# A spectral layer followed by an MLP on one core: prologue and first stages in another order, with products of zeros on TensorE

## The chip, the cores and the metric

The kernel runs on one core of a Trainium2 chip. The metric is the device time of one launch in microseconds (us), the median of several runs. TensorE (PE) multiplies matrices, VectorE (DVE), ScalarE (ACT) and GpSimd (POOL) work on elements, and SyncE (SP) issues transfers; each engine has an instruction queue of its own, in order, and waits for others by semaphores.

## The reference

Eight sequences of 3008 tokens with 256 features go through a linear layer in the frequency domain and then through an MLP. All results are float32; the weights of the MLP come as float64.

```python
X = np.fft.rfft(x, axis=1)
Xr, Xi = (X.real.astype(np.float32), X.imag.astype(np.float32))
Yr = Xr @ w_r - Xi @ w_i + b_r
Yi = Xr @ w_i + Xi @ w_r + b_i
lam = 0.01
Yr = np.sign(Yr) * np.maximum(np.abs(Yr) - lam, 0.0)
Yi = np.sign(Yi) * np.maximum(np.abs(Yi) - lam, 0.0)
Y = Yr.astype(np.float64) + 1j * Yi.astype(np.float64)
y = np.fft.irfft(Y, n=x.shape[1], axis=1)
...
h = x @ w_in
g = np.maximum(0.01 * h, h)
return (g @ w_out).astype(np.float32)
```

In the MLP x is y as 24064 tokens; w_in is 256 x 2048 and w_out 2048 x 256.

## The kernel before

**The transforms.** A transform of 3008 = 47 x 64 points is two stages of products with constant matrices. `fwd(b)` is stage A of batch b: it loads x in seven blocks ("chunks"; the tile is xin), adds and subtracts its two halves (`fold`, tile xs; DVE for batch 0, POOL later), multiplies by fa, copies the result to SBUF and stores it to DRAM as u_dram. `mid(b)` is the middle part: for 12 pairs of frequencies it loads u, does stage B (product with fb, L335), the linear layer (`proj`: three products with w_r, w_i - w_r and -(w_r + w_i), called wr, wd, wn), the threshold (tiles t and c), a copy with signs (zf), and the first stage of the inverse with gb (`stage_g`, here called the turn), and stores v_dram. `inverse` loads vin, multiplies by ga (L472), and gives y as chunks of 512 tokens (yc).

**The MLP ("MoE" in the names).** There are 47 chunks of tokens with 8 steps q each. It multiplies by a scheme of seven products in place of eight; `forms(ci)` makes its operands yh and yl out of yc (tile yt holds differences), as a rounded part and the rest. `moe_a` and `moe_b` multiply with w_in (`block`, L84: hi*hi, hi*lo, lo*hi), put the seven products together (p, u, gf) and apply the slope, and `moe_o` (L568) multiplies gh and gl with w_out two steps later. From batch 2 on the transforms are done with such split operands too: `split` in `fwd` makes xz, and `split_consts` splits wr, wd, wn, gb and fa into hi and lo (L104, L105). Batches 0 and 1 do stage A in plain float32, and batch 0 also the middle part.

**The weights.** w_in is loaded raw (win_raw) in four quarters (`load_win`) and turned to float32 by `convert_win`, 13 instructions on DVE for each; w_out is done in eight pieces by `load_wout`.

**The order.** Ahead of the MoE, `fwd(0)` runs, then `mid(0)` with the conversions of w_in laid between its steps, then `fwd(1)`, then the inverse and `forms` of chunk 0. The rest runs inside the MoE: a `Stream` is a generator with a total of columns, and `to(frac)` takes it on as far as the position in the MoE asks. The MoE is cut into stretches, numbered cur = 0 to 6, one for each middle part that remains; a stretch holds the streams in turn. Before, stretch cur has `fwd(cur + 2)` and then `mid(cur + 1)`, so that u of a batch is stored one stretch before it is read. `load(j)` at the start of `mid` fetches the first two u pairs.

**What sets an engine's order.** The program is written in one order for all engines, and a scheduler of the framework puts each engine's instructions in a row by its own simulated time; `tc.issue_after(ins)` adds an edge to that. Tiles of one tag share buffers; psh, psf and pso are the PSUM banks.

Of the kernel before, what the change touches and what calls it, by code (L numbers as in the profile page):

```python
# [8 lines left out]
F32 = mybir.dt.float32  # L9
# [9 lines left out]
N1, N2, NK1 = 47, 64, 24  # L19
# [11 lines left out]
def spectral_mlp_kernel(  # L31
# [171 lines left out]
    reads, written, turned, turning, thresholded = [], [], [], [], []  # L203
    NX = -(-NS // 2)
    XT = [("gf", 2)] + [("gl", 2)] * 2 + [("gh", 2)] * 2 + [("yc", 2)] * 2
    XT1 = [("yc", 2)] * 2 + [("gf", 2), ("gh", 2), ("yl", 2), ("yh", 2), ("gh", 2)]

    def fwd(b):
# [3 lines left out]
        x_t, s_t = {}, {}  # L212

        def load(c):
            cols = slice(2 * c * D, min(2 * c + 2, NS) * D)
            n = cols.stop - cols.start
            if b < NPRE:
                tag, bufs = (XT, XT1)[b][c]
                x2 = sb.tile([PA, 2, 2 * D], F32, name="xin", tag=tag, bufs=bufs)
                x_t[c] = [x2[:, h, :n] for h in range(2)]  # L220
            else:
                x_t[c] = [
                    sb.tile([PA, 2 * D], F32, name=f"xin{h}", tag="uv"[h], bufs=3 - h)[:, :n] for h in range(2)
                ]
            for h, t in enumerate(x_t[c]):
                if b == 0:
                    (act if h else sync).dma_start(t, x[b, h, :, cols])
                else:
                    with tc.issue_after(reads[-1].ins):
                        sync.dma_start(t, x[b, h, :, cols])  # L230
# [19 lines left out]
        def stage_a(c, h):  # L250
            t = x_t[c][h]
            n = t.shape[1]
            pa = (bank("psf", 2) if b else bank("psh", 4))[:PA, :n]
            products(pa, [(consts[f"fa{h}"] if b else consts[f"fa{h}32"], s_t[c][h])])
            t = x_t[c][1 - h]
            cp = act.copy(t, pa)
            if b == 0:
                turned[:] = [cp]
            st = (act if b else sync).dma_start(uv[h, :, 2 * c * D:2 * c * D + n], t)
            if b == 0:  # L260
                written.append(st)
# [22 lines left out]
        ahead = 2 if b >= NPRE else NX  # L284
        for c in range(ahead):
            load(c)
# [17 lines left out]
    def mid(b):  # L304
# [111 lines left out]
        yield 0  # L416
# [71 lines left out]
    def forms(ci):  # L488
# [7 lines left out]
        def split(k, w):  # L496
            act.copy(yh[:, k], w)  # L497
            return dve.tensor_sub(yl[:, k], w, yh[:, k].bitcast(F32))  # L498
# [12 lines left out]
        if ci == 0:  # L511
            made[:] = [last]
# [126 lines left out]

    fa32 = sb.tile([PA, 3, PA], F32, name="fa32", tag="xi", bufs=1)  # L640
# [7 lines left out]
    load_win(0, (sync, act))  # L648
    load_plain("fb", fb, [P, NK1 + 1, N2])
    load_weights()  # L650
# [6 lines left out]
    sync.dma_start(consts["gb32"][0], gb)  # L657
# [6 lines left out]
    load_win(1, (sync, sync), written[7])  # L664
# [4 lines left out]
    act.copy(bz[:1], brow[:1])  # L669
    act.copy(bz[32:33], brow[32:33])  # L670
    dve.tensor_sub(bz[32:33], brow[32:33], bz[32:33].bitcast(F32))
    act.mul(fa32[:, 2], fa32[:, 1], -1.0)
    convert_win(0)
    m0 = Stream(mid(0), MID)
    m0.to(0.001)
    for c in range(2, 4):
        load_win(c, (sync, sync), reads[3])
# [6 lines left out]
    with tc.issue_after(turned[0].ins):  # L684
        convert_win(1)
    wout = load_wout()
    for i in range(1, 17):
        m0.to(i / 16)
        if i in (3, 8):
            convert_win(2 + i // 8)  # L690
# [4 lines left out]
    m0.finish()  # L695
    fp.to(0.69)
# [5 lines left out]
    with tc.issue_after(thresholded[-1].ins):  # L702
        split_consts()
# [3 lines left out]
    next(wout)  # L707


    mids = [Stream(mid(b), MID) for b in range(1, NB)]  # L710
    cur, streams = -1, ()
    for i, pos in enumerate(moe()):
# [3 lines left out]
        if i in (2, 4):  # L716
            with tc.issue_after(made[0].ins):
                next(fp.gen)
        while cur + 1 < NB - 1 and pos >= (read[cur + 1] if cur >= 0 else 0):
# [3 lines left out]
            streams = ([Stream(fwd(cur + NPRE), FWD)] if cur + NPRE < NB else []) + [mids[cur]]  # L723
# [111 lines left out]
```

## Time and profile before

| | before |
| --- | --- |
| median of 3 runs | 2609.61 us (2607.25 to 2610.03) |
| profiled execution | 2609.83 us |
| its span, first to last instruction | 2608.0 us |
| PE busy | 2543.3 us (98%) |
| DVE busy | 1884.8 us (72%) |
| ACT busy | 1654.5 us (63%) |
| mean granted clock of TensorE | 0.991 |

The span is what the trace covers; 1.8 us of the execution lie outside it. PE idles for 64.7 us in all. The granted clock is a share of the full 2.4 GHz, so that 0.5 is the lower of the two levels. A window of the trace gives, for a stretch of time, how long each engine was busy and how many instructions it had.

### The profile page before, as it was taken

How to read it: one execution, taken by the hardware profiler on the slowest of the kernel's cores; microseconds unless marked ns; L12 is line 12 of the kernel's file. 1: busy time of each engine (PE TensorE's matmuls, PEld its weight loads, DVE VectorE, ACT ScalarE, POOL GpSimd, SP SyncE). 2: the span in 40 equal slices, each digit the busy share in tenths (PEclk: the TensorE clock that was granted, in tenths of full speed). 3: DMA queues.
4: the chain of work that ended last, by engine and by line, in shares of the span. 5: the costliest groups of instructions: out<-in, count | busy, mean ns of one | idle time of the engine just before them, and what ended most of it. 6: DMA issues, size and time to landing. Idle time of an engine off the chain costs nothing.

```text
span 2608.0 us, 42647 instructions
## 1 busy us (share of the span) xinstructions
PE 2543.3 (98%) x16300; PEld 2283.9 (88%) x16300; DVE 1884.8 (72%) x3403; ACT 1654.5 (63%) x3174; POOL 248.2 (10%) x180
## 2 busy tenths in 40 slices
PE   5899999999999999999999999999999999999999
PEld 3678887999989999899999999999999999989998
DVE  6697667777787777777777777777777767667665
ACT  4665665676656666567665766666666666655554
POOL 0002102100120001200021000211000000000000
PEclk8999999999999999999999999999999999999999
DMA  8634113211142112312123111231111111100000
GB/s 248 172 99 116 53 42 92 84 52 47 32 120 61 48 37 56 101 53 59 33 74 94 52 45 41 74 94 52 45 41 53 41 41 44 42 18 32 9 17 17
DMA packets 119914, 165.14 MB, mean 63 GB/s; under 512 B 13602, under 2 KB 69918, under 8 KB 119710
## 3 DMA queue, kind: packets, MB, share of 16 engines
q1 hardware_dynamic: 79120, 115.55, 14.5%
q10 hardware_dynamic: 40589, 46.87, 7.1%
q8 instruction: 128, 2.10, 0.3%
q14 instruction: 77, 0.62, 0.1%
HBM read 86.60 MB, written 75.76 MB: 62 GB/s over the span
## 4 chain that ended last, share of the span: by engine, by line
PE 90%; DVE 3%; ACT 3%; DMA 1%; issue 1%; ACTq 0%; SPq 0%; DVEq 0%
PE pso L568 38%; PE psh L84 34%; PE psf L78 11%; PE psf L472 3%; PE psf L335 3%; DVE gl L555 1%; ACT zf L392 0%; ACT gh L553 0%; ACT gf L551 0%; DMA u_dram<-xin 0%; DVE yl L498 0%; ACT zf L388 0%; DMA raw<-w_out_dram 0%; DVE gf L549 0%; ACTq L412 0%
## 5 line engine op out<-in xcount | busy, mean ns | idle before, releaser
L84 PE MATMUL psh<-yh,win_hi 128*128 128x256 f32 x2632 | 738.4, 285 | 8.1 <-ACT yh L497 4.1
L84 PE MATMUL psh<-yl,win_hi 128*128 128x256 f32 x2632 | 735.1, 281 | 0.0
L84 PE MATMUL psh<-yh,win_lo 128*128 128x256 f32 x2632 | 727.2, 280 | 0.0
L555 DVE TENSOR_TENSOR gl<-gf,gh 128x1024 fp32r<-128x1024 f32 x376 | 475.9, 1266 | 197.5 <-ACT gh L553 195.9
L568 PE MATMUL pso<-gh,wout_hi 128*128 128x512 f32 x1504 | 596.0, 396 | 1.9 <-ACT gh L553 1.8
L568 PE MATMUL pso<-gh,wout_lo 128*128 128x512 f32 x1504 | 591.3, 393 | 0.0
L568 PE MATMUL pso<-gl,wout_hi 128*128 128x512 f32 x1504 | 559.8, 396 | 2.7 <-DVE gl L555 2.4
L84 PEld LDWEIGHTS psh<-yh,win_hi 128*128 128x128 f32 x2632 | 494.3, 189 | 33.6 <-ACT yh L497 5.7
L84 PEld LDWEIGHTS psh<-yl,win_hi 128*128 128x128 f32 x2632 | 497.1, 189 | 25.8 <-issue 0.5
L84 PEld LDWEIGHTS psh<-yh,win_lo 128*128 128x128 f32 x2632 | 493.5, 189 | 4.0 <-issue 0.2
L551 ACT ACTIVATE gf<-gf 128x768 f32<-128x768 f32 x376 | 318.6, 848 | 216.3 <-DVE gf L549 211.3
L553 ACT CAST gh<-gf 128x1024 fp32r<-128x1024 f32 x376 | 395.5, 1052 | 16.5 <-ACT gf L551 10.5
L549 DVE TENSOR_TENSOR gf<-psh,u 128x512 f32<-128x512 f32 x376 | 258.9, 689 | 198.4 <-PE psh L84 196.6
L568 PEld LDWEIGHTS pso<-gl,wout_hi 128*128 128x128 f32 x1504 | 282.5, 188 | 60.7 <-DVE gl L555 7.9
L568 PEld LDWEIGHTS pso<-gh,wout_lo 128*128 128x128 f32 x1504 | 282.9, 188 | 45.1
L568 PEld LDWEIGHTS pso<-gh,wout_hi 128*128 128x128 f32 x1504 | 283.0, 188 | 41.2 <-ACT gh L553 3.0
L548 ACT ACTIVATE gf<-psh 128x256 f32<-128x256 f32 x376 | 144.4, 384 | 214.2 <-PE psh L84 193.0
L371 POOL TENSOR_TENSOR kb<-bias,kc 128x512 f32<-128x512 f32 x84 | 121.4, 1446 | 1468.3 <-ACT kc L368 1302.2
L534 ACT COPY p<-psh 128x256 f32<-128x256 f32 x376 | 139.5, 371 | 100.0 <-PE psh L84 82.2
L535 DVE TENSOR_TENSOR u<-psh,p 128x256 f32<-128x256 f32 x376 | 157.8, 420 | 60.8 <-ACT p L534 58.2
L537 DVE TENSOR_TENSOR gf<-psh,u 128x256 f32<-128x256 f32 x376 | 157.6, 420 | 22.3 <-PE psh L84 11.1
L538 DVE TENSOR_TENSOR gf<-psh,gf 128x256 f32<-128x256 f32 x376 | 158.0, 421 | 6.8
(134 smaller groups left out, 3290.9 us busy)
## 6 DMA issues: line engine op xcount, KB each, us to landing
u<-u_dram SPq DMA_DIRECT2D x192, 128.0 KB, 2.7
v_dram<-v ACTq DMA_DIRECT2D x192, 128.0 KB, 2.4
out_dram<-ob SPq DMA_DIRECT2D x94, 256.0 KB, 2.1
vin<-v_dram SPq DMA_DIRECT2D x96, 240.0 KB, 3.5
xin<-x_dram SPq DMA_DIRECT2D x90, 240.0 KB, 3.0
u_dram<-xin ACTq DMA_DIRECT2D x72, 240.0 KB, 2.4
u_dram<-xin SPq DMA_DIRECT2D x24, 240.0 KB, 4.6
raw<-w_out_dram SPq DMA_DIRECT2D x8, 512.0 KB, 4.9
```

The lines of the kernel that those rows point to most:

```text
L78: last = nc.tensor.matmul(dst, a, b, start=(i == 0), stop=(i == len(terms) - 1))
L84: nc.tensor.matmul(dst, a, b, start=start and i == 0, stop=i == 2, skip_group_check=True)
L534: act.copy(p1, b1[:, lo])
L535: dve.tensor_add(u2, b1[:, hi], p1)
L537: dve.tensor_add(g[:, 3], b2[:, hi], u2)
L538: dve.tensor_add(g[:, 3], b2[:, lo], g[:, 3])
L548: act.activation(g[:, 0], b1[:, lo], AF.Prelu, alpha=SLOPE)
L549: dve.tensor_add(g[:, 1:3], b2.rearrange("p (k n) -> p k n", k=2), u2.unsqueeze(1).broadcast_to([P, 2, HT]))
L551: act.activation(g[:, 1:4], g[:, 1:4], AF.Prelu, alpha=SLOPE)
L553: act.copy(gh, g)
L555: dve.tensor_sub(gl, g, gh.bitcast(F32))
L568: nc.tensor.matmul(po, a[:, f, s], r[:, i], start=(f == 0 and j == 0), stop=(f == NF - 1 and j == 2),)
```

## The change

- The four blocks of x of batch 0 are the column groups 0 to 2, 2 to 6, 6 to 10 and 10 to 13 of 13, in place of seven blocks of two groups; a store of u_dram is one for each half of a block.
- 10 products of zeros (128 x 240) stand at the start, 16 after the last product of stage A of batch 0.
- The loads of w_in's first quarters, of most of fb and of the weights go behind the stores of u_dram, and w_in and the rest of fb behind the first loads of u. `convert_win` moves with them: the first quarter into `mid(0)`, the last behind its last threshold.
- `split_consts` moves from behind the last threshold of `mid(0)` to the MoE's ninth half step, with edges to the end of `forms(0)`.
- Stage A of batch c + 1 now runs in the same stretch as its middle part, in stretches 1 to 6; stretch 0 has the middle part of batch 1 alone. `mid` gives 6 * CS columns after its first loads, which the totals count.

```diff
@@ -200,22 +200,37 @@
-    reads, written, turned, turning, thresholded = [], [], [], [], []
+    reads, written, turned, turning, thresholded, last_a = [], [], [], [], [], []
     NX = -(-NS // 2)
-    XT = [("gf", 2)] + [("gl", 2)] * 2 + [("gh", 2)] * 2 + [("yc", 2)] * 2
+    XW = [(0, 2), (2, 6), (6, 10), (10, 13)]
+    XT = ["gf", "gl", "gh", "yc"]
     XT1 = [("yc", 2)] * 2 + [("gf", 2), ("gh", 2), ("yl", 2), ("yh", 2), ("gh", 2)]
...
         uv = ud.rearrange("c k (g s) d -> c (k g) (s d)", g=NG)
-        x_t, s_t = {}, {}
+        x_t, s_t, wide = {}, {}, {}
...
             n = cols.stop - cols.start
+            if b == 0:
+                lo, hi = XW[c]
+                if c == 0:
+                    x2 = sb.tile([PA, 2, 2 * D], F32, name="xin", tag=XT[c])
+                    w = [x2[:, h] for h in range(2)]
+                else:
+                    w = [sb.tile([PA, 4 * D], F32, name="xin", tag=XT[c])[:, :(hi - lo) * D] for _ in range(2)]
+                for h, t in enumerate(w):
+                    (act if h else sync).dma_start(t, x[b, h, :, lo * D:hi * D])
+                for s in range(lo, hi, 2):
+                    x_t[s // 2] = [t[:, (s - lo) * D:min(s + 2 - lo, hi - lo) * D] for t in w]
+                    wide[s // 2] = (w, lo, hi, s + 2 >= hi)
+                return
             if b < NPRE:
-                tag, bufs = (XT, XT1)[b][c]
+                tag, bufs = XT1[c]
                 x2 = sb.tile([PA, 2, 2 * D], F32, name="xin", tag=tag, bufs=bufs)
@@ -223,11 +238,8 @@
             for h, t in enumerate(x_t[c]):
-                if b == 0:
-                    (act if h else sync).dma_start(t, x[b, h, :, cols])
-                else:
-                    with tc.issue_after(reads[-1].ins):
-                        sync.dma_start(t, x[b, h, :, cols])
+                with tc.issue_after(reads[-1].ins) if b == 1 else nullcontext():
+                    sync.dma_start(t, x[b, h, :, cols])
@@ -251,14 +263,16 @@
             pa = (bank("psf", 2) if b else bank("psh", 4))[:PA, :n]
-            products(pa, [(consts[f"fa{h}"] if b else consts[f"fa{h}32"], s_t[c][h])])
+            last_a[:] = [products(pa, [(consts[f"fa{h}"] if b else consts[f"fa{h}32"], s_t[c][h])])]
             t = x_t[c][1 - h]
             cp = act.copy(t, pa)
-            if b == 0:
-                turned[:] = [cp]
-            st = (act if b else sync).dma_start(uv[h, :, 2 * c * D:2 * c * D + n], t)
-            if b == 0:
-                written.append(st)
+            if b:
+                act.dma_start(uv[h, :, 2 * c * D:2 * c * D + n], t)
+                return
+            turned[:] = [cp]
+            w, lo, hi, last = wide[c]
+            if last:
+                written[:] = [sync.dma_start(uv[h, :, lo * D:hi * D], w[1 - h])]
@@ -281,8 +295,8 @@
-        ahead = 2 if b >= NPRE else NX
-        for c in range(ahead):
+        ahead = 2 if b else NX
+        for c in range(ahead if b else len(XW)):
             load(c)
@@ -413,7 +427,7 @@
             load(j)
-        yield 0
+        yield 6 * CS if b else 0
         if b:
@@ -494,8 +508,8 @@
         def split(k, w):
-            act.copy(yh[:, k], w)
-            return dve.tensor_sub(yl[:, k], w, yh[:, k].bitcast(F32))
+            cp = act.copy(yh[:, k], w)
+            return dve.tensor_sub(yl[:, k], w, yh[:, k].bitcast(F32)), cp
@@ -509,7 +523,7 @@
         if ci == 0:
-            made[:] = [last]
+            made[:] = last
         yield
@@ -637,6 +651,17 @@
+    zeros = sb.tile([P, NG * NK1 * 2], F32, name="zeros", tag="odd", bufs=1)
+    dve.memset(zeros, 0.0)
+    def idle(n):
+        t = bank("pso", 2)
+        for _ in range(n):
+            last = nc.tensor.matmul(t[:, :2 * NG * NK1], zeros[:, :P], zeros, start=True, stop=True)
+        return last
+    idle(10)
     fa32 = sb.tile([PA, 3, PA], F32, name="fa32", tag="xi", bufs=1)
@@ -645,69 +670,73 @@
     f0.to(0.01)
-    load_win(0, (sync, act))
-    load_plain("fb", fb, [P, NK1 + 1, N2])
-    load_weights()
+    consts["fb"] = const.tile([P, NK1 + 1, N2], F32, name="fb")
+    sync.dma_start(consts["fb"][:, :5], fb[:, :5])
     brow = sb.tile([P, 2 * D], F32, name="brow", tag="kb", bufs=1)
...
     sync.dma_start(sign, sg)
-    sync.dma_start(consts["gb32"][0], gb)
...
     f0.finish()
-    load_win(1, (sync, sync), written[7])
+    with tc.issue_after(last_a[0].ins):
+        idle(16)
+    with tc.issue_after(written[0].ins):
+        load_weights()
+        sync.dma_start(consts["gb32"][0], gb)
     pair("win", [P, 7, NQ, P])
...
         sb.tile([P, 4, 2, P], F32, name="ws", tag="yh"))
-    act.copy(bz[:1], brow[:1])
-    act.copy(bz[32:33], brow[32:33])
+    with tc.issue_after(turned[0].ins):
+        act.copy(bz[:1], brow[:1])
+        act.copy(bz[32:33], brow[32:33])
+        act.mul(fa32[:, 2], fa32[:, 1], -1.0)
     dve.tensor_sub(bz[32:33], brow[32:33], bz[32:33].bitcast(F32))
-    act.mul(fa32[:, 2], fa32[:, 1], -1.0)
-    convert_win(0)
     m0 = Stream(mid(0), MID)
     m0.to(0.001)
-    for c in range(2, 4):
-        load_win(c, (sync, sync), reads[3])
+    with tc.issue_after(reads[3].ins):
+        sync.dma_start(consts["fb"][:, 5:], fb[:, 5:])
+    load_win(0, (sync, sync), reads[3])
+    with tc.issue_after(turned[0].ins):
+        convert_win(0)
     bias = const.tile([P, 2, D], F32, name="bias")
...
     fp = Stream(fwd(1), FWD)
-    with tc.issue_after(turned[0].ins):
-        convert_win(1)
     wout = load_wout()
...
         m0.to(i / 16)
-        if i in (3, 8):
-            convert_win(2 + i // 8)
+        if i in (1, 5, 8):
+            load_win(1 + i // 4, (sync, sync), reads[-1])
+        if i in (5, 10):
+            convert_win(i // 5)
         if 5 <= i < 12:
...
     m0.finish()
+    with tc.issue_after(thresholded[-1].ins):
+        convert_win(3)
     fp.to(0.69)
...
             inverse(p, eh)
-    with tc.issue_after(thresholded[-1].ins):
-        split_consts()
     for _ in forms(0):
...
     next(wout)
-    next(wout)
-    mids = [Stream(mid(b), MID) for b in range(1, NB)]
+    mids = [Stream(mid(b), MID + 6 * CS) for b in range(1, NB)]
     cur, streams = -1, ()
@@ -716,11 +745,14 @@
                 next(fp.gen)
+        if i == 8:
+            with tc.issue_after(made[0].ins), tc.issue_after(made[1].ins):
+                split_consts()
         while cur + 1 < NB - 1 and pos >= (read[cur + 1] if cur >= 0 else 0):
...
             cur += 1
-            streams = ([Stream(fwd(cur + NPRE), FWD)] if cur + NPRE < NB else []) + [mids[cur]]
+            streams = ([Stream(fwd(cur + 1), FWD + 4 * CS)] if cur else []) + [mids[cur]]
         frac = (pos - read[cur]) / (read[cur + 1] - read[cur]) if cur + 1 < NB else 1
```

**SP at the end of stage A of batch 0.** Before, the stores of u_dram, loads of w_in (win_raw) and the first loads of u stand in this order:

```order
L259 DMA u_dram<-xin 120x512 x7
L147 DMA win_raw<-w_in_dram 128x1024
L259 DMA u_dram<-xin 120x512 x3
L147 DMA win_raw<-w_in_dram 128x1024
L259 DMA u_dram<-xin 120x512
L259 DMA u_dram<-xin 120x256 x2
L321 DMA u<-u_dram 64x2x256 x6
```

Of the changed kernel the same place (L275 is the store, L113 the weights w_r and w_i, L691 gb, L335 the load of u, L704 the rest of fb, L147 w_in):

```order
L275 DMA u_dram<-xin 120x512
L680 DMA sign<-sg_dram 128x36
L275 DMA u_dram<-xin 120x512
L275 DMA u_dram<-xin 120x1024 x4
L275 DMA u_dram<-xin 120x768 x2
L113 DMA w_192<-w_r_dram 128x2x256
L113 DMA w_i<-w_i_dram 128x2x256
L691 DMA w_192<-gb_dram 128x128
L335 DMA u<-u_dram 64x2x256 x6
L704 DMA fb<-fb_dram 128x1280
L147 DMA win_raw<-w_in_dram 128x1024 x2
L98 DMA ga<-ga_dram 120x256
```

No load of w_in stands ahead of the loads of u any more; the weights stand between the stores and the loads.

**ACT at the first products of the MoE.** Before, the casts yh of `forms(0)`, two copies of stage A of batch 1 (xin<-psf) and the first copies p, by which the seven products are put together:

```order
L497 CAST yh<-yc 128x512
L485 COPY yc<-y 128x428
L497 CAST yh<-yt 128x512
L497 CAST yh<-yc 128x512
L272 COPY xin<-psf 120x512 x2
L534 COPY p_937<-psh 128x256
L534 COPY p_993<-psh 128x256
L192 CAST wout_hi<-cva 128x512
L272 COPY xin<-psf 120x512 x2
```

Of the changed kernel (L511 is yh, L286 the copies of stage A, L104 the casts of `split_consts`, L548 the copy p):

```order
L511 CAST yh<-yt 128x512
L286 COPY xin<-psf 120x512 x4
L511 CAST yh<-yc 128x512
L104 CAST wr_hi<-w_192 128x512
L104 CAST wd_hi<-w_192 128x512
L104 CAST wn_hi<-w_192 128x512
L104 CAST gb_hi<-w_192 128x128
L104 CAST fa_hi<-fa_79 120x120 x2
L489 COPY odd<-psf 128x240
L548 COPY p_920<-psh 128x256
```

All four copies of stage A from psf and the casts of `split_consts` now stand ahead of the first p.

**PE at the end of a stage A inside the MoE.** Before, in stretch 0, the last products of stage A of batch 2 (xz) and the first of stage B of batch 1 (L335):

```order
L78 MATMUL psf<-xz,fa_hi 120x512
L78 MATMUL psf<-xz,fa_lo 120x512
L78 MATMUL psf<-xz,fa_hi 120x256 x2
L78 MATMUL psf<-xz,fa_lo 120x256
L78 MATMUL psf<-xz,fa_hi 120x256
L335 MATMUL psf<-fb,u 128x2x64 x4
L84 MATMUL psh<-yh,win_hi 128x256
L78 MATMUL psf<-xz,fa_hi 120x256
```

Of the changed kernel, the last products of xz (batch 2) and, behind the line of dots, the first of stage B (L349) of the same batch:

```order
L78 MATMUL psf<-xz,fa_hi 120x256
L78 MATMUL psf<-xz,fa_lo 120x256
L582 MATMUL pso<-gh,wout_hi 128x512
L582 MATMUL pso<-gh,wout_lo 128x512
...
L84 MATMUL psh<-yh,win_lo 128x256
L84 MATMUL psh<-yh,win_hi 128x256
L84 MATMUL psh<-yl,win_hi 128x256
L84 MATMUL psh<-yh,win_lo 128x256
L349 MATMUL psf<-fb,u 128x2x64 x4
L486 MATMUL psf<-ga,vin 128x128 x4
```

The two stages of one batch follow each other directly, with 27 products of the MoE (L582 with w_out, L84 with w_in) between them, where before stage B used a u that had been stored a stretch earlier. In the five later stretches 51, 43, 47, 45 and 47 products lie between.

## Rows read from the trace of the kernel before

**Rows 1.** Windows: length, then PE, PEld, DVE, ACT, POOL busy; clock, DMA share, GB/s.

```profile
25.00:41.60 16.60, 0.00 (x0) 0.02 (x1) 9.64 (x14) 6.56 (x11) 0.00 (x0) 0.55 0.74 245
41.60:50.00 8.40, 8.39 (x39) 8.09 (x40) 6.34 (x12) 3.79 (x6) 0.00 (x0) 0.67 0.93 308
50.00:100.00 50.00, 47.19 (x243) 38.46 (x243) 40.35 (x70) 40.01 (x82) 0.30 (x1) 1.00 0.67 180
100.00:110.00 10.00, 4.61 (x10) 1.88 (x9) 4.90 (x11) 4.03 (x10) 0.00 (x0) 0.76 0.36 84
110.00:130.00 20.00, 20.00 (x74) 11.18 (x74) 10.11 (x20) 11.18 (x24) 0.00 (x0) 0.95 0.71 218
130.00:150.00 20.00, 17.03 (x99) 12.40 (x97) 15.90 (x36) 12.68 (x29) 0.00 (x0) 1.00 0.60 183
...
230.00:250.00 20.00, 16.21 (x83) 13.01 (x82) 14.68 (x29) 11.30 (x24) 5.08 (x4) 0.91 0.50 144
...
300.00:320.00 20.00, 15.31 (x83) 13.07 (x82) 12.36 (x25) 13.23 (x31) 2.09 (x2) 0.83 0.28 85
...
380.00:390.00 10.00, 6.29 (x36) 5.61 (x35) 5.42 (x12) 6.69 (x16) 0.00 (x0) 0.83 0.23 77
...
440.00:455.00 15.00, 11.00 (x51) 8.71 (x50) 11.78 (x22) 6.73 (x16) 3.46 (x4) 0.77 0.60 184
...
600.00:2600.00 2000.00, 1998.03 (x13083) 1818.79 (x13082) 1441.50 (x2606) 1276.96 (x2436) 179.51 (x126) 1.00 0.18 51
```

**Rows 2.** Waits of PE: line waited for, us in total, times, longest.

```profile
PE psh L335 <- DMA u<-u_dram: 18.9, 2, 17.3
...
PE psf L78 <- DVE xz L246: 5.1, 4, 2.4
...
PE psf L78 <- DVE yt L503: 4.0, 1, 4.0
```

**Rows 3.** Timeline of PE: start us, us, what ran, idle before.

```profile
7.16 2.06 PE L78 MATMUL psh<-xs,fa 120*120 120x512 f32 x2 [7.16 <-DVE xs L237]
...
13.57 1.02 PE L78 MATMUL psh<-xs,fa 120*120 120x512 f32 x2
...
41.61 3.76 PE L335 MATMUL psh<-fb,u 128*128 128x128 f32 x16 [17.31 <-DMA u<-u_dram]
...
107.85 2.05 PE L78 MATMUL psh<-zf,w 128*128 128x512 f32 x2 [4.39 <-DVE zf L390]
```

**Rows 4.** Timeline of DVE, at stage A and from the last turn on.

```profile
11.24 0.69 DVE L237 TENSOR_TENSOR xs<-xin 120x512 f32<-120x512 f32 x1 [0.98 <-DMA xin<-x_dram]
...
104.50 0.69 DVE L105 TENSOR_TENSOR wr_lo<-w,wr_hi 128x512 fp32r<-128x512 f32 x1
...
106.99 0.71 DVE L390 TENSOR_SCALAR zf<-t,sign 64x256 f32<-64x256 f32 x2
...
128.25 0.41 DVE L498 TENSOR_TENSOR yl<-yc,yh 128x256 fp32r<-128x256 f32 x1
...
147.57 0.69 DVE L549 TENSOR_TENSOR gf<-psh,u 128x512 f32<-128x512 f32 x1
```

**Rows 5.** Timeline of SP's DMA issues ahead of the first u.

```profile
31.64 1.63 SPq L259 DMA_DIRECT2D u_dram<-xin  x3
37.88 3.95 SPq L321 DMA_DIRECT2D u<-u_dram  x6
```

**Rows 6.** Timeline of ACT at the first products of the MoE.

```profile
133.84 0.61 ACT L497 CAST yh<-yt 128x512 fp32r<-128x512 f32 x1
...
134.88 1.06 ACT L272 COPY xin<-psf 120x512 f32<-120x512 f32 x2
```

**Rows 7.** The page's DMA issues: count, KB each, median us to landing.

```profile
u<-u_dram SPq DMA_DIRECT2D x192, 128.0 KB, 2.7
...
u_dram<-xin ACTq DMA_DIRECT2D x72, 240.0 KB, 2.4
u_dram<-xin SPq DMA_DIRECT2D x24, 240.0 KB, 4.6
```

## The prediction, before the changed kernel had run

> **What bounds the kernel now.** I read the busy times stretch by stretch first, then what TensorE waited for, then the timelines of the stretches that are not full. From 600 to 2600 us TensorE is busy 1998.03 of 2000 us at a granted clock of 1.00 [rows 1]; nothing can be won there without taking products out, and none are taken out. All that can move lies before 600 us. There three places stand out. In 25.00:41.60 TensorE does nothing: a wait of 17.3 us for u from DRAM [rows 2], after which its first product of the middle part starts at 41.61 [rows 3]; it then works at a clock of 0.67 [rows 1]. In 100:110 it is busy 4.61 us, the last turn product (zf, w) being late. And at three later places, 230:250, 300:320 and 380:390, it is idle for 3.79, 4.69 and 3.71 us, and the granted clock is 0.91, 0.83 and 0.83, which in 20, 20 and 10 us costs 1.8, 3.4 and 1.7 us more [rows 1]: 19.1 us in all. A fourth such place, 440:455, has 4.00 us idle and a clock of 0.77 (3.5 us).
>
> The two clock levels are seen in one product: the pair of 512-column products of stage A takes 2.06 us in the row at 7.16 and 1.02 us at 13.57 [rows 3]: half of 2.4 GHz, then all of it. A wait thus costs itself and the half rate behind it: mean (1.8 + 3.4 + 1.7 + 3.5)/4 = 2.6 us.
>
> **1. Earlier start of the middle part: -11.8 us.** Before, the third x block is taken by VectorE at 11.24 us [rows 4], stage A ends at 41.61 - 17.31 = 24.3 [rows 3], and the stores of u go out on SP with loads of w_in between them, the last group of stores at 31.64 lasting 1.63, so until 33.3; the loads of u are issued at 37.88 [rows 5]. From the last store issue to the first product it is 41.61 - 33.3 = 8.3 us. In the changed kernel the second block holds two chunks; with the first it has as many bytes as three blocks of before, the third of which was taken at 11.24, and in fewer and longer rows, so I put its landing at 10.5. Then 5.5 pairs of chunks at half rate: a 512-column product is 1.71 us there (0.855 at full rate, from the starts of the rows at 7.16 and 13.57), 5.5 x 1.71 = 9.4, stage A ends at 20.3 (19 to 21.3). The eight merged stores follow their block, the last is issued 1.2 us later, 21.5. I keep the 8.3 us: start 29.8. Bounds: 28.5, if the smaller traffic ahead shortens the 8.3; 32, if the three loads of weights queued right behind the stores on SP slow the loads of u. So -11.8 (-13 to -9.6).
>
> **2. The middle part itself: 0.** Before it lasts from 41.61 to 107.85 + 2.05 = 109.9, 68.3 us. Gain: the zeros after stage A keep TensorE busy 16 x 0.4 = 6.4 us (half a 512-column product each, 0.4 at full rate) until about 26.7, three us ahead of its operands. The clock lost 0.33 x 8.39 = 2.8 us in 41.60:50.00 [rows 1]; I take half, -1.4 (0 to -2.8). Gain: the six subtractions of the split weights, from 104.50 to 106.99 in VectorE's row ahead of the last zf [rows 4], leave that path: -2.5. Loss: w_in's first quarter now lands only after the loads of u, with the rest of fb: 1.7 MB at 245 GB/s [rows 1] behind 29.8, at 36.7. From there to the last sign copy the new order has 87 instructions on VectorE; at 40.35/70 = 0.576 us [rows 1] this is 50.1 us, and at the share that VectorE had, 40.35/50 = 0.81, 62 us, until 98.6. That is 29.8 + 68.8, just the length of before: VectorE takes back the 3.9 us, so +4 (0 with VectorE never idle, +9 if a load of w_in is late by the 4 to 5 us of the slowest rows [rows 7]). Sum 0 (-4 to +5).
>
> **3. Stage A of batch 1 at full rate: -2.** The product at 107.85 takes 2.05 us for what is 1.02 at the full clock [rows 3], as the wait ahead of it is gone; 0.05 x 20 us in 110:130 is another 1.0 [rows 1]. Bounds 0 and -3: it is lost whole if a new wait comes in the last turns.
>
> **4. First MoE steps: +6.** The split of the constants is not dropped but moved to the first w_in products. Between the first yl at 128.25 and the second gf at 147.57 + 0.69 VectorE has 34 instructions, 20.0 us, 0.59 each [rows 4]; now 40, so +3.5. ScalarE gets six casts and two more psf copies ahead of the first p copy: the wide cast is 0.61 and a copy 0.53 [rows 6], four wide casts or copies and the small ones make about 2.5 us. The casts' matmul cover is thin: before, products of stage A stood between the first steps and filled the waits; in the new order eight come in one run. In 130:150 VectorE was 15.9 of 20 us busy [rows 1] and TensorE already lost 3 there. Bounds 0 (all of it in those idle times) and +10.
>
> **5. The three borders: -12.** In them the MoE, the middle part of batch 1 and stage A of batch 2 meet on VectorE; the changed first stretch has no stage A. The waits are for VectorE (yt 4.0 us, xz 5.1 in four [rows 2]), and xz is stage A's own split. But yt belongs to the forms of the next chunk, which stay. I take two thirds of the 19.1 us: -12 (-18 to -4). The place at 440:455 stays, since there a stage A and the middle part still meet.
>
> **6. Handover from stage A to the middle part: +3.** Before, u of a batch is stored one stretch ahead of its use. Now fwd(c+1) and mid(c+1) follow each other within a stretch, six times. A copy (0.5 to 0.6 [rows 6]), a store of 2.4 and a load of 2.7 [rows 7] in series, with about 1 for issues: 6.7 us from the last product of stage A to the first of stage B. What TensorE has there instead is read from the order: 27, 51, 43, 47, 45 and 47 products of the MoE and of stage A; one is 1998.03/13083 = 0.153 us [rows 1], so 4.1, 7.8, 6.6, 7.2, 6.9 and 7.2. Only the first is clearly short, by 2.6. I take +3; bounds 0 and +15, since the margins of the other five are under 1.2 us.
>
> **Sum.** -11.8 + 0 - 2 + 6 - 12 + 3 = -16.8; the profiled execution of before has 2608.0 in the span and 1.8 outside it, 2609.8, which is 0.2 above the median of the runs shown. 2609.8 - 16.8 = **2593**.
>
> The Trainium skill, TensorE: Matmul & The Clock Gate, Part 1: The HAM clock gate, says that the array is throttled by default and that sustained activity releases it; the zeros are that activity, and by it the term in point 2 would be the full -2.8, the time 2591.6. The trace agrees as far as it goes: 0.55 in the idle 25.00:41.60 and 0.67 behind it.
>
> **Rivals.** (a) The first MoE steps hide the split and the borders vanish: -6 and -6 on the sum, 2581. For it: the idle time of VectorE in 130:150; against it: four consumers wait there in a chain. Chance 0.25. (b) The borders are not won: the wait for yt is there whoever works beside it, so the 12 us stay, and the handover costs 5: 2607. For it: yt is the longest of the three waits; against it, xz. Chance 0.17. (c) Slower: the handover. If the store and load go as in the beginning, 4.6 for a store of u and 2.7 for a load [rows 7], with two issues of the six that took 3.95 [rows 5], the way is 0.6 + 4.6 + 2.7 + 1.3 = 9.2 us; less the cover, the six waits are 5.1 + 1.4 + 2.6 + 2.0 + 2.3 + 2.0 = 15.4 us, and behind each the clock falls, at the 2.6 us of the borders: 15.6. That is 31.0 in place of 3: **2621**. It decides from about 22 us of handover on. Against it: in the MoE stretch the queues move 51 GB/s, at the beginning 245 [rows 1]. Chance 0.08. The Trainium skill, DMA: Bandwidth & Descriptors, Latency and other measured facts, lists HBM access as slower under high load and as the main part of a transfer's fixed cost; at 51 GB/s it gives this rival little. Forecast: 0.5.
>
> **Numbers.** The forecast's own range is 2584 to 2602, from the bounds of terms 4 to 6. The 80% range 2577 to 2608 takes in (a) with two more us of borders each, and (b); it leaves out (c) and the outer parts. A difference of 0.2%, 5.2 us, is about what this kernel's measurement can tell from none: faster than 2604.4 are (a), the forecast but for its upper edge (0.48) and a third of (b), 0.25 + 0.48 + 0.06 = 0.79; slower than 2615 is (c), 0.08; the rest is 0.13.
>
> **What would show it.** Right: the first stage B product at 29 to 31 us with a granted clock above 0.8 behind it; no subtraction of split weights before the last zf; stage A of batch 1 at 1.02 us a pair of products; at the old places of 230, 300 and 380 at least two without idle time; a wait of TensorE for u of 2 to 3 us in the second stretch and hardly any later. Wrong: waits for u in all six stretches with half rate behind them (c); a long wait for p or yl near 120 to 140 us (term 4 too small); waits for yt as before (b). A time over 2608 means that the gain at the start was given back in the middle part, where VectorE would be the row to look at.

## The result, and the profile after

The changed kernel takes 2616.61 us (median of 8 runs, 2614.73 to 2618.49), the kernel before 2609.42 us beside it: the ratio is 1.003, with a 95% interval of 1.0019 to 1.0041. It is slower by 7.2 us, where 16.8 less were forecast.

What of it lies where, the profile after tells. The windows first, with the stretches of [rows 1] that were forecast to move (the columns are the same):

```profile
27.00:32.40 5.40, 1.06 (x7) 0.67 (x5) 1.29 (x2) 0.00 (x0) 0.00 (x0) 0.97 0.78 246
32.40:50.00 17.60, 16.34 (x87) 14.27 (x88) 9.38 (x16) 7.83 (x15) 0.00 (x0) 0.91 0.95 277
50.00:100.00 50.00, 41.29 (x200) 31.58 (x199) 42.88 (x75) 42.85 (x83) 0.31 (x1) 0.97 0.66 191
...
121.50:153.00 31.50, 25.05 (x118) 18.94 (x117) 23.66 (x56) 21.11 (x48) 0.00 (x0) 0.84 0.34 102
...
230.00:250.00 20.00, 20.00 (x141) 18.58 (x140) 16.39 (x32) 14.97 (x32) 1.30 (x1) 1.00 0.20 55
300.00:320.00 20.00, 18.45 (x116) 16.65 (x115) 14.57 (x27) 13.74 (x29) 1.54 (x2) 0.91 0.21 66
380.00:390.00 10.00, 10.00 (x63) 8.91 (x62) 7.39 (x12) 7.93 (x14) 2.60 (x2) 1.00 0.07 22
440.00:455.00 15.00, 15.00 (x93) 13.36 (x92) 9.60 (x18) 8.09 (x14) 1.49 (x2) 1.00 0.18 51
600.00:2600.00 2000.00, 1992.05 (x12918) 1801.87 (x12917) 1415.58 (x2601) 1263.06 (x2414) 189.46 (x139) 1.00 0.18 53
```

The wait of 17.3 us ahead of the first stage B is 4.3 us now, with the zeros in 6.6 us of the time ahead of it. Of the four borders three are full, 440:455 among them, where no gain was forecast; 300:320 still has 1.55 us idle and a clock of 0.91. But 121.50:153.00, the first MoE steps, has 6.45 us idle at a clock of 0.84, and the last row, where nothing was expected, holds 7.95 us idle where [rows 1] has 1.97, and 165 products fewer in the same 2000 us. TensorE's waits (line waited for, us in total, times, longest):

```profile
PE psh L78 <- ACT zf L406: 8.2, 5, 3.6
PE psh L349 <- DMA u<-u_dram: 5.6, 2, 4.3
PE psh L84 <- DVE u L549: 4.8, 4, 2.8
```

Of the timeline of TensorE: the end of stage A of batch 0 with the zeros behind it, the first stage B, the last turns, the first MoE product and the first with w_out.

```profile
20.94 0.59 PE L78 MATMUL psh<-xin,fa 120*120 120x256 f32 x2
21.37 6.64 PE L661 MATMUL pso<-zeros 128*128 128x240 f32 x32
32.36 3.52 PE L349 MATMUL psh<-fb,u 128*128 128x128 f32 x16 [4.34 <-DMA u<-u_dram]
...
99.63 3.78 PE L78 MATMUL psh<-zf,w 128*128 128x512 f32 x4 [3.61 <-ACT zf L406]
...
121.53 0.36 PE L84 MATMUL psh<-yh,win_hi 128*128 128x256 f32 x1
...
151.76 0.40 PE L582 MATMUL pso<-gh,wout_hi 128*128 128x512 f32 x1
```

Stage B starts 9.2 us earlier than at 41.61 [rows 3], the MoE 8.2 us earlier than before (129.77), and the first product with w_out comes at 151.76 where it came at 150.21: all of the lead is gone in 30 us. One trace of each kernel carries a spread of its own: among traces with the same order of instructions up to there, the first MoE product starts at 121.53, 120.15 and 123.12 us (the changed kernel and the runs e1 and e6 below) and at 129.77, 127.22 and 132.82 (before, e5 and e9). A difference of 3 us at this place between two traces shows nothing by itself.

From there on one follows the chunks. The table gives the start of the last product with gl of a chunk, in us from the span's start, read from the timelines; e1 to e15 are the experiments told below.

| | before | after | e3 | e8 |
| --- | --- | --- | --- | --- |
| chunk 0 | 192.0 | 200.7 | 193.5 | 193.4 |
| chunk 9 | 727.5 | 705.7 | 691.6 | 691.5 |
| chunk 34 | 2049.3 | 2024.1 | 2009.3 | 2009.4 |
| chunk 40 | 2350.4 | 2342.1 | 2326.1 | 2328.1 |
| chunk 45 | 2565.6 | 2569.2 | 2552.5 | 2544.4 |
| last | 2603.9 | 2612.4 | 2596.7 | 2582.9 |
| us a chunk, 40 to 45 | 43.0 | 45.4 | 45.3 | 43.2 |

At chunk 34 the changed kernel is 25.2 us ahead. A part of that is only put off, as a stage A runs a stretch later: behind chunk 34 the products of the transforms take 50.7 us before and 65.4 us after (each from its start to the next start, at most 1 us), 14.7 us more, so 10.5 us are won. At the end it is 8.5 us behind: 19 us are lost in the last twelve chunks, 12 of them between chunks 40 and 45, where of the transforms only the last products of the inverse are left (about 6 us in both) and the diff touches nothing.

### The profile page after: what moved, and what is told of

It is laid out like the page before. It is cut to its first block, busy times and chain, and to the rows that moved or that the text cites. A ratio compares the mean times of both kernels' runs of the same rounds, so it can differ in the third digit from the quotient of the medians.

```text
span 2616.4 us, 42725 instructions
## 1 busy us (share of the span) xinstructions
PE 2570.9 (98%) x16352; PEld 2298.7 (88%) x16352; DVE 1856.5 (71%) x3404; ACT 1655.8 (63%) x3174; POOL 236.9 (9%) x180
## 5 line engine op out<-in xcount | busy, mean ns | idle before, releaser
L84 PE MATMUL psh<-yh,win_hi 128*128 128x256 f32 x2632 | 738.4, 285 | 8.7 <-DVE u L549 4.8
L84 PE MATMUL psh<-yl,win_hi 128*128 128x256 f32 x2632 | 738.1, 282 | 1.4 <-DVE yl L512 1.4
L84 PE MATMUL psh<-yh,win_lo 128*128 128x256 f32 x2632 | 729.4, 282 | 0.0
L582 PE MATMUL pso<-gh,wout_hi 128*128 128x512 f32 x1504 | 597.8, 398 | 5.9 <-ACT gh L567 3.8
L569 DVE TENSOR_TENSOR gl<-gf,gh 128x1024 fp32r<-128x1024 f32 x376 | 465.9, 1240 | 193.6 <-ACT gh L567 192.0
L582 PE MATMUL pso<-gh,wout_lo 128*128 128x512 f32 x1504 | 592.1, 394 | 0.0
L582 PE MATMUL pso<-gl,wout_hi 128*128 128x512 f32 x1504 | 557.9, 397 | 3.9 <-DVE gl L569 2.5
L84 PEld LDWEIGHTS psh<-yh,win_hi 128*128 128x128 f32 x2632 | 494.6, 189 | 33.6 <-DVE u L549 5.6
L84 PEld LDWEIGHTS psh<-yl,win_hi 128*128 128x128 f32 x2632 | 498.2, 189 | 24.7 <-DVE yl L512 2.4
L84 PEld LDWEIGHTS psh<-yh,win_lo 128*128 128x128 f32 x2632 | 493.7, 189 | 3.1
L567 ACT CAST gh<-gf 128x1024 fp32r<-128x1024 f32 x376 | 394.5, 1050 | 14.9 <-ACT gf L565 9.8
L582 PEld LDWEIGHTS pso<-gl,wout_hi 128*128 128x128 f32 x1504 | 282.3, 188 | 69.5 <-DVE gl L569 14.6
L582 PEld LDWEIGHTS pso<-gh,wout_hi 128*128 128x128 f32 x1504 | 282.8, 188 | 51.1 <-ACT gh L567 10.0
L582 PEld LDWEIGHTS pso<-gh,wout_lo 128*128 128x128 f32 x1504 | 282.9, 188 | 48.6
L548 ACT COPY p<-psh 128x256 f32<-128x256 f32 x376 | 139.4, 371 | 102.0 <-PE psh L84 93.8
```

Source lines behind the costliest of these rows:

```text
L84: nc.tensor.matmul(dst, a, b, start=start and i == 0, stop=i == 2, skip_group_check=True)
L548: act.copy(p1, b1[:, lo])
L567: act.copy(gh, g)
L569: dve.tensor_sub(gl, g, gh.bitcast(F32))
L582: nc.tensor.matmul(po, a[:, f, s], r[:, i], start=(f == 0 and j == 0), stop=(f == NF - 1 and j == 2),)
```

## The experiments

**The last chunks.** The order of instructions shows what is new there. In chunks 39 to 46 of the changed kernel VectorE does the steps of the MoE two at a time, both sums gf<-psh,u and then both remainders gl; the kernel before does so throughout in chunks 38 to 40 (and in 15 and 27, far from the end). Of ScalarE's timeline in the changed kernel (start, us, what ran, idle before):

```profile
2499.49 0.37 ACT L548 COPY p<-psh 128x256 f32<-128x256 f32 x1 [1.25 <-PE psh L84]
2502.79 1.58 ACT L565 ACTIVATE gf<-gf 128x768 f32<-128x768 f32 x2 [2.93 <-DVE gf L563]
2504.28 1.03 ACT L567 CAST gh<-gf 128x1024 fp32r<-128x1024 f32 x1
2505.22 0.36 ACT L548 COPY p<-psh 128x256 f32<-128x256 f32 x1
2505.48 1.05 ACT L567 CAST gh<-gf 128x1024 fp32r<-128x1024 f32 x1
```

ScalarE idles 2.93 us and then has two steps at once. TensorE at the same place:

```profile
2504.94 0.28 PE L84 MATMUL psh<-yh,win_lo 128*128 128x256 f32 x1
2505.36 0.50 PE L582 MATMUL pso<-gh,wout_hi 128*128 128x512 f32 x1
...
2506.16 0.39 PE L582 MATMUL pso<-gh,wout_lo 128*128 128x512 f32 x1
2506.62 0.50 PE L582 MATMUL pso<-gl,wout_hi 128*128 128x512 f32 x1
```

It starts with gh 0.42 us after the start of the product ahead (0.12 is the pace there), and with gl after 0.46 (pace 0.23), every second step. The edit puts the steps in a row:

```diff
-        product(b2[:, hi], ci, q, 4)
+        prev[:] = [product(b2[:, hi], ci, q, 4)]
...
-            moe_a(ci, q)
+            with tc.issue_after(prev[0].ins) if ci >= 38 else nullcontext():
+                moe_a(ci, q)
```

> The changed kernel with one edge more: from chunk 38 of the MoE on, the first products of a step (moe_a) stand behind the last products of the step before (moe_b) on TensorE. Theory T (the time is lost in the last nine chunks, where the order now bunches two steps, and not where the change was made): the chunks 39 to 45 take 43.0 us each as before and not 45.4, TensorE has hardly any idle time after 2000 us, and the time is 2616.6 - 20, 2594 to 2600. Rival U (the last chunks are slower for another reason, such as transfers or buffers that come free late, and the bunched order is only seen beside it): 2613 or more, and the waits for gh and gl stay.

2601.7 us, 14.9 less than the changed kernel and 0.9974 of before (0.9964 to 0.9984). The windows of 2400 to 2570 us, of the changed kernel and of this one:

```profile
2400.00:2570.00 170.00, 167.46 (x1029) 146.08 (x1028) 100.91 (x186) 87.56 (x155) 0.00 (x0) 1.00 0.04 13
```

```profile
2400.00:2570.00 170.00, 170.00 (x1085) 154.20 (x1084) 114.89 (x198) 95.23 (x164) 0.00 (x0) 1.00 0.04 13
```

Not a wait is left, and 56 products more are done in the same time; a chunk takes 43.3 us. U falls; the gain was some microseconds under what I had set. The same edge on the kernel before:

> The kernel before with the edge of the first run alone (from chunk 38 on, moe_a behind the moe_b of the step before). In its own order only chunks 38 to 40 are bunched, so by theory T the edge takes 2 us for two or three chunks and nothing after: 2603 to 2609. Rival U2 (the edge is worth its 13 to 15 us whatever the order was, so the bunching is no cause): 2593 to 2597.

2608.2 us, 0.9995 (0.9987 to 1.0004). The edge is worth nothing where the order was not bunched, so U2 falls too.

**Stretches and prologue apart.** Two kernels, each with one of the two. The edit of the first, e2; the second, e3, has the same lines the other way round in the kernel before:

```diff
-        yield 6 * CS if b else 0
+        yield 0
...
-    mids = [Stream(mid(b), MID + 6 * CS) for b in range(1, NB)]
+    mids = [Stream(mid(b), MID) for b in range(1, NB)]
...
-            streams = ([Stream(fwd(cur + 1), FWD + 4 * CS)] if cur else []) + [mids[cur]]
+            streams = ([Stream(fwd(cur + NPRE), FWD)] if cur + NPRE < NB else []) + [mids[cur]]
```

> The changed kernel with the stretches as before (stage A of batch c + 2 with the middle part of batch c + 1, no columns after the first loads, totals as before); the whole new prologue, the zeros and the moved split stay. Theory T (the new stretches win about 18 us between 150 and 600 us and lose 21 us or more in the last chunks, the new prologue gains nothing by 150 us): the last chunks as before, the borders as before, so 2605 to 2612. Rival V (the prologue wins, as was forecast, about 8 us, and the stretches lose all that is lost): 2599 to 2603. Rival W (the prologue is what loses): 2615 or more.

2629.3 us, 1.0074 (1.006 to 1.0087): W's time, with the last chunks in their old order at 43.3 us.

> The kernel before with the new stretches alone (stage A of batch c + 1 with the middle part of the same batch, 6 * CS columns after the first loads, new totals); prologue, split and all else as before. Theory T: its last eight chunks stand in the bunched order of the changed kernel, so they take 45.4 us each; the borders are won: 2611 to 2619. Rival W (the prologue loses): 2600 or less, with the last chunks at 43 us.

2601.9 us, 0.9973 (0.9963 to 0.9982). Theory T had the parts wrong in both, and W, by which the prologue loses, was nearer (in e3 it missed the bunched chunks): the prologue is a loss, of 14.7 (after less e3) to 20.3 us (e2 less before), and the stretches win 7.1 us although their last chunks are bunched (45.3 us each). So it is the new stretches that bunch the tail, with either prologue; and with the edge on e3 they should win much more:

> The kernel before with the new stretches and with the edge of the first run (from chunk 38 on, moe_a behind the moe_b of the step before); old prologue, old places. If the parts add up: 2601.9 less what the edge won in the changed kernel, 14.9: 2585 to 2590. If the tail's gain was bound to the changed prologue: 2600 to 2603.

2588.8 us, 0.9922 (0.9908 to 0.9935): the tail's price is 13.1 us here, and the new stretches with the tail in order win 20.2 us. This is the fastest kernel of the study. Its windows at the old borders:

```profile
230.00:250.00 20.00, 19.94 (x135) 17.99 (x134) 13.27 (x24) 11.90 (x26) 2.41 (x2) 1.00 0.18 46
300.00:320.00 20.00, 19.84 (x132) 18.19 (x133) 15.40 (x27) 12.63 (x27) 3.75 (x2) 1.00 0.23 67
380.00:390.00 10.00, 10.00 (x62) 8.82 (x62) 8.29 (x14) 4.93 (x8) 3.94 (x3) 1.00 0.35 92
440.00:455.00 15.00, 15.00 (x93) 13.35 (x92) 8.87 (x16) 8.14 (x14) 0.00 (x0) 1.00 0.18 50
```

**A slower pace everywhere.** Between 600 and 2000 us the products of yl with win_hi are followed by the next after 0.1175 us in the mean in before and e3, and after 0.1187 us in the changed kernel, e1, e2 and e4 (from the starts in the timelines, gaps over 0.4 us left out). Steady, without a wait, and with the new prologue only. What that changes for all later work is where tiles lie: the pool gives places as tags are first asked for, and in the new prologue this order differs; by the sizes in the two lists of tags, yh lies 15424 bytes lower in a partition, and w_out and others move too. So the tags were asked for ahead of all work, in the other kernel's order, with every instruction in its place (the traces show the same order on every engine). The list for the kernel before:

```diff
+    for tag, n, bufs in (
+        ("odd", 240, 1), ("xi", 360, 1), ("yl", 1792, 2), ("gf", 1024, 2),
...
+    ):
+        for _ in range(bufs):
+            sb.tile([P, n], F32, name="place", tag=tag, bufs=bufs)
```

> The kernel before, every instruction in the same order on every engine, but its tiles at the places in SBUF that they have in the changed kernel (the pool gives places in the order in which tags are first asked for; here the tags are asked for once ahead of all work, in the changed kernel's order). Theory P (the place of the operands sets the pace of the products: 600 to 2000 us, the products of yl with win_hi follow each other at 0.1175 us in the two kernels with the places of before and at 0.1187 us in the kernels with the changed prologue): 7896 products of the first MoE matrix are 0.0012 us slower each, 9.5 us, the products with wr, wd and wn gain some 2 us: 2615 to 2618. Rival Q (the slower pace comes with something else of the new prologue, such as its transfers or the number of instructions): 2607 to 2611, pace 0.1175.

2615.3 us, 1.0023 (1.0014 to 1.0033), pace 0.1186.

> The changed kernel with its instructions in the same order, and its tiles at the places in SBUF of the kernel before. Theory P: pace 0.1175 us, 2607 to 2611. Rival Q: 2615 to 2618, pace 0.1187.

2610.95 us, 1.0006 (0.9997 to 1.0014), pace 0.1178. P holds both ways, with 6.4 and 5.7 us. (The later runs with the new prologue and the old places, e10 and e14, have 0.1177 and 0.1174.) The same number of products of yl on the page of before, of e5 and of e6 (busy, mean ns of one):

```profile
L84 PE MATMUL psh<-yl,win_hi 128*128 128x256 f32 x2632 | 735.1, 281 | 0.0
```

```profile
L84 PE MATMUL psh<-yl,win_hi 128*128 128x256 f32 x2632 | 737.4, 282 | 0.0
```

```profile
L84 PE MATMUL psh<-yl,win_hi 128*128 128x256 f32 x2632 | 734.2, 281 | 1.2 <-DVE yl L512 1.2
```

One nanosecond in 281 looks like nothing; the windows of 600 to 2000 us show it better, before and e5, whose orders are the same: 34 products fewer at 0.153 us, 5.2 us.

```profile
600.00:2000.00 1400.00, 1398.26 (x9189) 1274.24 (x9188) 1035.98 (x1868) 914.88 (x1765) 164.03 (x115) 1.00 0.21 60
```

```profile
600.00:2000.00 1400.00, 1398.09 (x9155) 1272.89 (x9154) 1033.76 (x1864) 911.97 (x1760) 163.43 (x115) 1.00 0.21 59
```

Which tile's place it is, was not tried.

**The first MoE steps.** Two edits bear on them: the moved split, and a piece of w_out that is no longer converted ahead of the MoE.

```diff
+    with tc.issue_after(thresholded[-1].ins):
+        split_consts()
     for _ in forms(0):
...
-        if i == 8:
-            with tc.issue_after(made[0].ins), tc.issue_after(made[1].ins):
-                split_consts()
```

> The changed kernel with the split of the constants back at its old place, behind the last threshold and ahead of the last zf. Theory S (the moved split costs at the first MoE steps, as term 4 of the prediction has it, 6 us, and gains 2.5 us in the last turn): 2611 to 2614. Rival S0 (the first steps wait for the last quarter of w_in, which the change converts behind the middle part, and for w_out; the split is not what they wait for): 2615 to 2620.

2611.2 us, 1.0007 (0.9998 to 1.0016): 5.4 us less, S's number. But the edit did more than it says. Without the edges to `forms(0)` the scheduler puts ACT's cast of fa, which is part of the split, at the very start, where it waits for fa; ACT's later loads of x stand behind it. ACT in e7 and, in the last line, in the changed kernel:

```profile
1.82 1.28 ACT L104 ACT_TABLE_LOAD   x1 [1.82 <-POOL zero L323]
3.63 0.29 ACT L104 CAST fa_hi<-fa 120x120 fp32r<-120x120 f32 x1 [0.53 <-DMA fa<-fa_dram]
3.64 1.66 ACTq L227 DMA_DIRECT2D xin<-x_dram  x3
...
1.82 3.60 ACTq L227 DMA_DIRECT2D xin<-x_dram  x3
```

VectorE takes up the second block of x at 14.22 in place of 10.05 us, and stage B starts at 35.41 in place of 32.36. The kernel before has this cast at 11.58, behind its loads of x. So the 5.4 us are what the split costs at the MoE, less a start that is some 3 us later; e10, e14 and e15 below have the cast at the start too (stage B at 37.75, 36.73 and 36.05). A kernel with the old split and the cast behind the loads was not tried.

```diff
     next(wout)
+    next(wout)
```

> The changed kernel with one edit undone that the prediction gave no term: the second piece of w_out is again converted ahead of the MoE (the second call of its generator behind the forms of chunk 0). Theory O (one piece less ahead leaves the conversions of w_out two half steps later beside the first chunks, where VectorE is busy 46 of 50 us from 150 to 200 us, and puts the steps of the first chunks in another order): 2610 to 2613. Rival O0 (a conversion costs VectorE the same 4.5 us ahead of the MoE or in it): 2615 to 2619.

2611.6 us, 1.001 (1.0001 to 1.0019): 5.0 us, as O has it. By the traces chunk 0 ends 5.0 us earlier (195.7 and 200.7); the order of the MoE's steps differs from there to about 1850 us, so not all of the 5.0 need come from the first chunk.

**The zeros.**

```diff
-    idle(10)
...
-    with tc.issue_after(last_a[0].ins):
-        idle(16)
```

> The changed kernel without the 26 products of zeros. Theory T: the zeros act on the first 50 us alone; stage A is slower by its first half rate (some 4 us more for 5 pairs of products) and the start of the middle part by up to 3 us, and both vanish in the wait for the last turns, where VectorE and ScalarE end last: 2615 to 2621. If the clock at the start counts in full: 2621 to 2625.

2624.2 us, 1.0059 (1.0046 to 1.0071): they win 7.6 us in the changed kernel, more than T allowed; the other reading, the clock at the start in full, had the number. The trace does not bear it out as the whole cause: the first stage B starts at 32.23 us without the zeros and at 32.36 with them, the granted clock from 32 to 50 us is 0.89 and 0.91, and the first MoE product comes 3.3 us later (124.80 and 121.53). Another 3.5 us are lost from the first product with gl to the end of chunk 0 (51.5 and 48.0 us), and there the order of instructions is another one too, up to 237 us.

**The parts together.**

> The changed kernel with three things undone at once: the tail in order as in the first run, the places in SBUF of before, the split of the constants at its old place. If the three losses add up: 2616.6 - 14.9 - 5.7 - 5.4 = 2590.6, 2588 to 2594. What then is left of the new prologue (the later loads of w_in and fb, the wide blocks, the zeros) is worth nothing beside the old prologue, 2588.8. If they overlap: 2596 or more.

2592.3 us, 0.9933 (0.9919 to 0.9946). The three losses add up to within 2 us (with the cast of fa at the start, as told).

> The kernel of e10 with the loads of w_in, fb and the weights and the conversions of w_in in the old order (two quarters of w_in loaded ahead of u, the first converted before the middle part); the wide blocks of x, the merged stores of u and the zeros stay. Theory L (the late w_in is what makes the middle part longer and the first MoE steps later, and eats what the earlier start wins): 2580 to 2586. Rival L0 (VectorE has the same work either way, and the earlier start is what is worth something): 2592 or more.

2599.4 us, 0.9959 (0.9947 to 0.9972). L falls, and L0 has the number: the late loads win 7.1 us. Stage B starts at 37.75 us in e10 and at 44.34 in e11, the time from there to the last turn product is 69.6 and 69.2 us, and from the MoE's first products on (126.93 and 133.96) the order is the same on every engine: an earlier start counts in full here.

> The kernel of e10 (tail in order, old places, old place of the split) with the second piece of w_out ahead of the MoE. By its traces e10 writes its first w_out products 4 us ahead of e8 (147.1 and 151.3 us) and ends 3.4 us behind it, with 3.2 us idle between 150 and 200 us. Theory O: the lead of 4 us stays, 2583 to 2587. Rival O0: 2590 to 2594.

2590.5 us, 0.9929 (0.9916 to 0.9941): O falls, and O0 has the number. The 1.8 us, less than the 5.0 of e13, lie within the intervals of the two. Its MoE starts at 128.3, that of e8 at 130.3, and its first products with gl come at 153.5, those of e8 at 151.3.

> The kernel of e14 without the 26 products of zeros. By e4 (the changed kernel without zeros was 7.6 us slower): 5 to 8 us above e14. By e12 (36 and 10 zeros in the old prologue gave nothing): within 2 us of e14.

2593.8 us, 0.9941 (0.9928 to 0.9955): 3.2 us, between the two theories; the two intervals overlap. From 128 us on the order is the same in both, and the first MoE products come at 128.27 and 131.13.

> The kernel of e8 (old prologue, old places, new stretches, tail in order) with zeros, 10 ahead of stage A and 36 behind it. By the zeros' worth in the changed kernel (7.6 us) as an upper end, and the clock of 41.6 to 50 us alone (2.8 us) as a lower: 2581 to 2586. If the zeros act only where the wait is shorter: 2588 to 2590.

2590.8 us, 0.9928 (0.9916 to 0.9941), 2 us above e8: the zeros win nothing in the old prologue. There stage B starts 2.1 us earlier with them (40.2 and 42.4 us), no more than traces of this prologue differ by, and the last turn product is no earlier (111.0 and 108.5).

## Why the prediction was wrong, point by point

**The step that failed** is the first: "nothing can be won there without taking products out, and none are taken out. All that can move lies before 600 us". Nothing could be won there, but 20 us could be lost. The tail's bunched order (13.1 to 14.9 us) and the places (5.7 to 6.4 us) had no term, no rival and no place in the range; without the two, 2616.6 - 20 is about 2597, near the 2593 forecast. That nearness is luck: terms 1 to 4, the prologue, were put at -7.8 and cost, places taken off, 9.0 (14.7 - 5.7) to 13.9 us (20.3 - 6.4), and terms 5 and 6 were put at -9 and win 20.2. The order of instructions that the prediction read for three places had the bunched steps to show in its last rows; the prediction reads nothing there. It has no word on places in SBUF. Its last sentence, that a time over 2608 would mean the gain given back in the middle part, failed with it.

**Term 1**, -11.8: measured -9.2 (41.61 to 32.36), just outside its bounds. The 8.3 us from the end of the store issues to the first product came out at 8.2; what was mis-sized is the end of the store issues, 24.2 us on SP in place of 21.5. Stage A ended at 21.5 and not at 20.3, and the eight merged stores took SP until 2.7 us behind that, not 1.2. The weights behind them lasted to 27.4, and SP waited 0.4 us more for a store to land before the loads of u at 27.86, so the weights held them up by little, if at all. The 9.4 us in the sum is also called half rate and is not: 11 products of 0.855 us, at the full rate, take it. With the zeros ahead they did run at the full rate, in 10.7 us.

**Term 2**, 0: the first stage B to the last turns took 2.7 us longer (41.6 to 108.8 before, 32.4 to 102.3 after, starts of the first and the last product), within the bounds and within what traces of one order differ by (67.2 in before, 70.1 in e9). The clock of 0.91 in 32.40:50.00 costs 1.6 us of the 2.8, about the half that was taken. What ends it is ScalarE's zf, with VectorE 42.9 and ScalarE 42.9 of 50 us busy.

**Term 3**, -2: from the last turn to the first MoE product 20.9 us before, 19.2 after: -1.7.

**Term 4**, +6: from the first MoE product to the first with gl 22.3 us before, 31.2 after: 8.9, within the bounds, and 6 us more to the end of chunk 0 (42.0 us in e3, 48.0 after). The split was put too low: in e7's trace this stretch takes 20.2 us, so the split costs it 11.0. (The profiled executions of the two lie 10.4 us apart, their medians 5.4, with e7's later start in it.) The w_out piece, in the diff of the change and in no term, is another 5.0 in the changed kernel. Terms 1 to 4 each came out 0.3 to 2.9 us above the forecast, 8.4 in all: the -7.8 that they add up to is +0.6 at the first product with gl (152.08 before, 152.69 after).

**Terms 5 and 6**, -12 and +3: by e8 the new stretches win 20.2 us, so the gain was put at less than half. The wait for yt was not the forms' alone: without a stage A beside the first middle part it vanishes too, and so does 440:455; of the waits for xz 2.0 us are left, at 420 us. The handover costs next to nothing; TensorE waited for u inside the MoE once, 0.4 us. Rival (c), the prediction's way to a slower kernel, was the wrong one. The range is not worked out there either: the bounds of terms 4 to 6, added up, give 2578 to 2617 and not 2584 to 2602.

**The sum of what was measured**: -20.2 for the stretches with the tail in order, +1.7 for the rest of the new prologue (e14 less e8), +1.8 for the w_out piece (e10 less e14), +5.4, +5.7 and +14.9 for split, places and tail: +9.3, beside +7.2 measured. The 1.7 and the 1.8 are within the noise, and the w_out piece and the split act on the same steps, so their prices depend on what else is undone.

**What stays open**: why e10 and e14, whose stage B starts 4.6 and 5.7 us before that of e8, end no earlier. A part is the cast of fa, which takes some 4 us of the changed kernel's earlier start from them. What start is left does count in full between e10 and e11. The middle part is not shown to take it back: it lasts 70.8 us in e14 and 66.1 in e8, but e9, with the prologue of e8, has 70.1, and e11, with the old places of w_in's conversions, 69.2. What the traces of these two show is that the w_out piece is paid for in one place or the other: with the piece converted ahead of the MoE, in e14, the time from the first MoE product to the first with gl is 25.3 us (20.1 in e10), and with it inside, in e10, the time from there to the end of chunk 0 is 48.1 us (42.0 in e14); e8, with the piece ahead, has 21.0 and 42.1. Why the old prologue pays neither is open.

## What to carry to other kernels

Where a scheduler sets the order, an edit at the start can change the order of the end: read the last steady part of the new order as closely as the edited place, and compare the time of one period there. An allocation order is part of a change; hold tiles at their places before two versions are compared. An edit that is undone need not bring the old order back, as e7 shows. And a gain at the start has to be followed from stage to stage: here 9.2 us at the first stage B were 8.2 at the first MoE product and nothing at the first product with gl.

## What the runs showed of the hardware that was not expected

The pace of the same products in the same order depends on where their operands lie in SBUF: 0.1175 against 0.1186 us for a product of 256 columns, 6 us in 2609. And 26 products of zeros in idle time were worth 7.6 us in the changed kernel and 3.2 in e14, and 46 in the old prologue nothing; in the first of these the order of other instructions changed with them, so that the 7.6 are not theirs alone.
